# Two transform stages as 64x64 tiles: batches 2 to 7 of a Fourier mixing and feed-forward kernel

## The chip, the core and the metric

The kernel runs on one core of a Trainium2 chip. The core has a matrix engine (TensorE, "PE" in the profile, whose weight loads are shown apart as "PEld"), VectorE (DVE), ScalarE (ACT), GpSimd (POOL), a queue processor that here only issues transfers (SP), and sixteen DMA engines. The metric is the device time of one execution in microseconds (us); a kernel's time is the median of several runs.

## The reference

For every batch the sequence is filtered in the frequency domain, and the result goes through a two-layer network with a leaky ReLU:

```
x: (8, 3008, 256)    filt_r, filt_i: (1505, 256)    w_in: (256, 2048)    w_out: (2048, 256)
X = rfft(x, axis=1)
y = irfft(X * (filt_r + 1j * filt_i), n=3008, axis=1)
h = y.reshape(24064, 256) @ w_in
out = maximum(0.01 * h, h) @ w_out
```

## The kernel before

**The transform.** 3008 is 94 x 32, so each Fourier transform is made of two stages of small matrices. The kernel calls the four stages of a batch 1 to 4. Stage 1 (`s1_group`, line 254; its matmul is line 259) multiplies by the 94-point matrix: 16 groups a batch. Stage 2 (`s2_group`, line 302; matmul on line 308) multiplies by the 32-point matrix with the twiddle factors built in: 24 column blocks `c`, each with a weight matrix of its own (`f2_sb[:, c]`), 12 groups of two blocks a batch. Each block holds, on 128 partitions, the real and imaginary parts of two of the frequencies k1 side by side, and the weights are 128x128 with half of their entries zero, because the two frequencies do not mix. After stage 2 comes the product with the filter. Stage 3 (`sa_group`, line 326; matmul on line 330) goes back through the 32-point matrix, one matmul of 512 columns for each of the 12 groups, and its weights are again half zero. Stage 4 (`sb_group`, line 343; matmul on line 351) goes back through the 94-point matrix into `yt`, 16 groups a batch.

**The product with the filter.** It is complex: DVE multiplies the stage-2 result in PSUM by `fb_sb` into `p2` (line 317) and by `fa_sb` into `p1` (line 320); two transfers on SP swap the partition halves of `p2` into `p3` (lines 318 and 319), so that real parts meet imaginary parts; POOL adds `p1` and `p3` into `y` (line 323). `fb_sb` already holds the signs. The filter is loaded once at the start by POOL transfers that also convert float32 to float16 (line 204).

**Transposes.** Between stages 1 and 2 the data go through a DRAM tile `dz1` (stores from line 264, loads `t1_load`, line 268, into the ring `z1`), between stages 3 and 4 through `dz2` (stores from line 334, loads `t2_load`, line 275, into the ring `z2`). Both rings lie in the tile `big`.

**The network.** The 24064 tokens are taken in 47 chunks of 512. `moe1` (line 504) multiplies a chunk by `w_in`: 16 column tiles, two matmuls each (line 514), and after every second tile ACT applies the leaky ReLU to a pair of PSUM banks (line 519). The second layer is one chunk behind. From chunk 3 on it uses a seven-product scheme on quarters (matmuls of line 589; sums on DVE, lines 555 and 617 to 654).

**PSUM.** Two wide tiles (`ph`, two banks each) take turns for `moe1`. Two single banks (`pf`) serve the transform stages; `bank` (line 156) picks the one that by its own estimate (`frees`) comes free first. Two more hold the products of the second layer.

**The order.** The first batch is written out by hand as a list of steps (line 466). All that follows is put on a heap with a time and emitted in the order of these times (`at`, `work`). Time is counted in units, eight to a chunk. `plan` (line 694) gives each transform group of batches 1 to 7 a wished time; the loop from line 741 moves groups so that they stand at least `GAP` apart and after the transfers they need, with fixed allowances (`LANDED`, `READ`, `AFTER`). So each engine's order, and that of SP's and POOL's queues, is fixed when the program is built. An instruction whose data are late holds up everything behind it on its engine or queue.

In the first batch, stage 2 (`s2p`, line 390) also has matmuls with 128x64 weights, line 401: the two halves of the output partitions are made by two matmuls. Line 397 is the same with full weights.

Of the kernel before, what the change touches and what calls it, by code (L numbers as in the profile page):

```python
# [11 lines left out]
P = 128  # L12
FP16 = mybir.dt.float16
# [7 lines left out]
NC = 24  # L21
Q = 32
R1 = 96
FP = 3


def _build_np_constants(N):
    n1, n2 = np.arange(N1), np.arange(N2)
    h = N2 // 2

    k2 = np.concatenate([np.arange(h), np.arange(N2 - 1, h - 1, -1)])

    sg = np.where(k2 < h, 1.0, -1.0)[None, :]
    th = 2 * np.pi * np.outer(n2, k2) / N2
    co, si = np.cos(th), np.sin(th)

    fwd1 = np.zeros((P, P))
    fwd2 = np.zeros((P, NC, P))
    inv1 = np.zeros((P, N2, N1))
    inv2 = np.zeros((P, P))  # L40

    for s, (qr, qi) in enumerate(((0, 2), (1, 3))):
        k1 = NC * s + np.arange(NC)

        cr, ci = (slice(64 * i + s, 64 * i + 64, 2) for i in range(2))
        r, i = (slice(Q * q, Q * q + Q) for q in (qr, qi))
        ang = 2 * np.pi * np.outer(n1, k1) / N1
        fwd1[:N1, qr * Q : qr * Q + NC] = np.cos(ang)
        fwd1[:N1, qi * Q : qi * Q + NC] = -np.sin(ang)
        for c in range(NC):  # L50
            t = th + 2 * np.pi * n2[:, None] * k1[c] / N
            fwd2[r, c, cr], fwd2[i, c, cr] = np.cos(t), np.sin(t)
            fwd2[r, c, ci], fwd2[i, c, ci] = -np.sin(t) * sg, np.cos(t) * sg

        w = np.where((k1 == 0) | (k1 == N1 // 2), 1.0, 2.0)[:, None] / N1
        for j in n2:
            t = ang.T + 2 * np.pi * j * k1[:, None] / N
            inv1[qr * Q : qr * Q + NC, j, :] = w * np.cos(t)
            inv1[qi * Q : qi * Q + NC, j, :] = -w * np.sin(t)
        inv2[cr, r], inv2[ci, r] = co.T, -(si * sg).T  # L60
        inv2[cr, i], inv2[ci, i] = si.T, (co * sg).T
    inv2 /= N2


    inv2r = np.concatenate([inv2[:64], -inv2[:64]], axis=0)
    inv2i = np.concatenate([inv2[64:], inv2[64:]], axis=0)
    small = np.stack([fwd1, inv2, inv2r, inv2i], axis=1)

    fwd2t = fwd2.reshape(4, Q, NC, P).transpose(1, 0, 2, 3).reshape(P, NC, P)
    inv1t = inv1.reshape(4, Q, N2, N1)[:, :NC].transpose(1, 0, 2, 3).reshape(4 * NC, N2, N1)  # L70
    fwd2 = fwd2.reshape(P, FP, NC // FP, P).transpose(1, 0, 2, 3)
    return tuple(np.ascontiguousarray(t).astype(np.float16) for t in (fwd2, inv1, small, fwd2t, inv1t))


@with_exitstack
def kernel(
# [28 lines left out]
    REST = (5.37, 14.61, 8.86, 10.48, 23.53, 20.72)  # L105
    DUE = (3.52, 0.66)
    TWICE = (2.2, 2.35)
    F2T = 3.24
    LEAD = (3.85, 7.37)
    AFTER = (0.53, 0.8, 1.33, 3.17, 0.39, 0.52)  # L110
# [2 lines left out]
    PLANS = (  # L113
# [4 lines left out]
    )  # L118

    f2_np, i1_np, small_np, f2t_np, i1t_np = _build_np_constants(N)  # L120
    f2_d = nc.inline_tensor(f2_np, name="fwd2_const")
    i1_d = nc.inline_tensor(i1_np, name="inv1_const")
    small_d = nc.inline_tensor(small_np, name="small_const")
    f2t_d = nc.inline_tensor(f2t_np, name="fwd2t_const")
    i1t_d = nc.inline_tensor(i1t_np, name="inv1t_const")

    cpool = ctx.enter_context(tc.tile_pool(name="const", bufs=1))
    f2_sb = cpool.tile([P, NC, P], FP16, name="f2_sb")
# [3 lines left out]
    fb_sb = cpool.tile([P, NC, D], FP16, name="fb_sb")  # L132
    w_in_sb = cpool.tile([P, NDT, DFF], FP16, name="w_in_sb")
    w_out_sb = cpool.tile([P, NCT, D], FP16, name="w_out_sb")
    wt_sb = cpool.tile([P, 4, NCH, P], FP16, name="wt_sb")
    x_sb = cpool.tile([P, N2, D], FP16, name="x_sb")
    big = [cpool.tile([P, Q * D], FP16, name=f"big{i}") for i in range(3)]
# [31 lines left out]
    def at(time, f):  # L169
        clock["n"] += 1  # L170
        heapq.heappush(work, (time, clock["n"], f))
# [8 lines left out]
    def noted(what, f):  # L180
        f()
        issued.add(what)
# [58 lines left out]
    def turned(t, n, c):  # L241

        base = t[:]
        return bass.AP(tensor=base.tensor, offset=base.offset + 4 * c * D,
                       ap=[[P * D, n], [Q * D, 4], [1, 4 * D]])
# [22 lines left out]
    def t1_load(b, c):  # L268
        def go():
            need(*[("st1", b, h) for h in range(8)], *[("s2", b, 2 * c - 7)] * (c > 3))  # L270
            nc.sync.dma_start(z1[c % 4], turned(dz1[b % 2], N2, c))
            issued.add(("z1", b, c))
        return go

# [51 lines left out]
    def sa_group(b, g):  # L326
        def go():
            ps = bank("pf", 2, D)
            need(("y", b, g), *[("st2", b, g // 2 - 4)] * (g > 7))
            nc.tensor.matmul(ps, inv2, ys.pop((b, g))[:], start=True, stop=True)  # L330
            h = g // 2
            nc.scalar.copy(st2[h % 4][:, ds(2 * (g % 2), 2), :], ps)  # L332
            if g % 2:
                soon(AFTER[4], lambda: noted(("st2", b, h), lambda: nc.sync.dma_start(
                    dz2[b % 2][ds(4 * h, 4)].rearrange("k p d -> p k d"), st2[h % 4])))
        return go

    def quad_copy(h, dt, ps, copy):

# [164 lines left out]
    def moe1(ci, ct):  # L504
        g, j = divmod(ct, 2)
        if ct == 0:
            gts[ci] = gtp.tile([P, NCT, CH], FP16, tag="gt", name=f"gt_c{ci}")
        if j == 0:
            phs[0] = bank("ph", 2, CH)
        ph, t = phs[0], ci * CH  # L510
        while t < (ci + 1) * CH:
            e = min((ci + 1) * CH, (t // N + 1) * N)
            for dt in range(NDT):
                nc.tensor.matmul(ph[:, j, ds(t - ci * CH, e - t)], w_in_sb[:, dt, ts(ct, P)],  # L514
                                 yt[:, dt, ds(t % N, e - t)],
                                 start=(dt == 0), stop=(dt == NDT - 1))
            t = e
        if j == 1:
            nc.scalar.activation(gts[ci][:, ds(2 * g, 2), :], ph, AF.Lrelu)  # L519
# [174 lines left out]
    def plan(b, s1, s1_step, s2, s2_step, lag, sb, sb_step, xl, x_step):  # L694
        for g in range(16):
            groups.append((s1 + s1_step * g, 1, b, g, s1_group(b, g, dve if b == 1 and g % 4 < 3 else act)))
            if g % 2 and b + 1 < B:
                at(s1 + xl + x_step * g, lambda g=g: (need(("s1", b, g)), noted(
                    ("x", b + 1, g // 2), lambda: x_load(b + 1, 2 * g - 2, 4))))
        for g in range(12):  # L700
            groups.append((s2 + s2_step * g, 2, b, g, s2_group(b, g)))
            groups.append((s2 + lag + s2_step * g, 3, b, g, sa_group(b, g)))
        first_use[1, b], first_use[3, b] = s2, sb
        for g in range(16):
            due = SL * (QT * (8 * b + g // 2) // CH)
            groups.append((min(sb + sb_step * g, due - DUE[0] + DUE[1] * (g % 2)), 4, b, g, sb_group(b, g, act)))
# [21 lines left out]
    def load_time(stage, b, c):  # L728
# [7 lines left out]
            at(t, (t1_load if stage == 1 else t2_load)(b, c))  # L736
        return loads[stage, b, c]

    queue = [(time, n, *v) for n, (time, *v) in enumerate(groups)]
    heapq.heapify(queue)  # L740
    while queue:
        time, n, stage, b, g, f = heapq.heappop(queue)
        t = max(time, last + GAP)
        if stage == 3:
            behind = when[2, b, g] + y_delay(b, g) + 0.02 if (2, b, g) in when else None
        else:
            behind = load_time(stage - 1, b, g // 2) if stage != 1 else 0
            if stage != 1 and behind is not None:
                behind += READ
        if behind is None or behind + 0.02 > t:  # L750
            heapq.heappush(queue, (t + GAP if behind is None else behind + 0.03, n, stage, b, g, f))
            continue
        when[stage, b, g] = last = t
        at(t, f)
        if stage in (2, 4) and g % 2:
            place[stage - 1, g // 2 % 4] = t + 0.1
        assert stage < 4 or t < SL * (QT * (8 * b + g // 2) // CH), (b, g, t)

    for ci in range(NCHUNK + 1):
        if ci < NCHUNK:  # L760
            for ct in range(NCT):
                at(SL * ci + 0.5 * ct, lambda ci=ci, ct=ct: moe1(ci, ct))
        if ci == 0:
            continue
        wino = W0 <= ci - 1
        items = products(ci - 1) if wino else plain(ci - 1)
        for i, f in enumerate(items):
            at(SL * (ci + i / len(items)) + 0.01, f)
        if wino:
            for time, *what in [(v, i) for i, v in enumerate(SUMS)] if ci < NCHUNK else LAST:  # L770
                at(SL * ci + time, lambda ci=ci, what=what: act_sums(ci - 1, *what))
# [33 lines left out]
```

## Time and profile before

| | us |
|---|---|
| median of three runs | 748.61 |
| lowest and highest | 748.29, 750.29 |
| the profiled execution | 747.4 |
| its span, first to last instruction | 745.2 |
| granted TensorE clock | 0.999 of full |

The busy times of the profile's first part are unions over instructions. TensorE's matmuls are pipelined, so the mean duration of one is longer than its step in the stream. The chain of waits goes back from the last instruction to whatever released it; for a stream of matmuls it shows each one's step. DMA "share" is the mean busy share of the sixteen engines.

The groups that the change touches, beside those of lines 308 and 330, are these in the profile's list by form:

```profile
L332 ACT CAST big<-pf 128x512 f16<-128x512 f32 x84 | 49.0, 584 | 4.9 <-PE pf L330 3.0
L320 DVE TENSOR_TENSOR p_b_g<-pf,fa_sb 128x512 f32<-128x512 f32 x84 | 57.2, 681 | 0.2
L323 POOL TENSOR_TENSOR y_b_g<-p_b_g,p_b_g 128x512 f16<-128x512 f32 x84 | 116.4, 1388 | 414.9 <-DMA p_b_g<-p_b_g 249.9
```

The columns are the line, engine and operation, output and inputs, the count, the busy time with the mean in ns of one, and the engine's idle time just before with what ended most of it. There are 84 because batches 1 to 7 have twelve groups each.

### The profile page before, as it was taken

How to read it: one execution, taken by the hardware profiler on the slowest of the kernel's cores; microseconds unless marked ns; L12 is line 12 of the kernel's file. 1: busy time of each engine (PE TensorE's matmuls, PEld its weight loads, DVE VectorE, ACT ScalarE, POOL GpSimd, SP SyncE). 2: the span in 40 equal slices, each digit the busy share in tenths (PEclk: the TensorE clock that was granted, in tenths of full speed). 3: DMA queues.
4: the chain of work that ended last, by engine and by line, in shares of the span. 5: the costliest groups of instructions: out<-in, count | busy, mean ns of one | idle time of the engine just before them, and what ended most of it. 6: DMA issues, size and time to landing. Idle time of an engine off the chain costs nothing.

```text
span 745.2 us, 19416 instructions
## 1 busy us (share of the span) xinstructions
PE 738.0 (99%) x8017; PEld 528.9 (71%) x8017; DVE 504.6 (68%) x686; ACT 559.1 (75%) x755; POOL 166.2 (22%) x171
## 2 busy tenths in 40 slices
PE   9999999999999999999999999999999999999997
PEld 3556667677687777877778777777777777777776
DVE  5987637766776766766777667766677676465566
ACT  4776787888878787877777787787777777777762
POOL 6503412332232212121232222121212210000000
PEclk9999999999999999999999999999999999999999
DMA  9997797888876666655675656543554333111012
GB/s 207 229 224 197 191 224 216 209 195 208 216 181 147 159 186 176 169 138 163 193 178 150 159 155 175 156 139 109 144 160 119 106 103 103 60 55 55 29 46 70
DMA packets 119848, 113.64 MB, mean 152 GB/s; under 512 B 16384, under 2 KB 93056, under 8 KB 119568
## 3 DMA queue, kind: packets, MB, share of 16 engines
q1 hardware_dynamic: 104425, 94.73, 42.9%
q0 software_dynamic: 15056, 17.49, 15.8%
q8 instruction: 62, 1.02, 0.6%
q14 instruction: 26, 0.21, 0.1%
q10 hardware_dynamic: 279, 0.19, 0.1%
HBM read 57.51 MB, written 50.33 MB: 145 GB/s over the span
## 4 chain that ended last, share of the span: by engine, by line
PE 96%; DMA 1%; DVE 1%; ACT 1%; issue 0%; ACTq 0%; DVEq 0%
PE ph L514 43%; PE pf L589 18%; PE po_ps L589 18%; PE pf L259 3%; PE pf L351 3%; PE pf L308 2%; PE pf L330 2%; PE po_ps L373 1%; PE pf L681 1%; PE po_ps L681 1%; DMA dz<-big 1%; DMA big<-dz 0%; ACT yt L341 0%; PE pf L442 0%; PE ph L401 0%
## 5 line engine op out<-in xcount | busy, mean ns | idle before, releaser
L519 ACT ACTIVATE gt_c<-ph 128x1024 f16<-128x1024 f32 x376 | 385.3, 1025 | 133.5 <-PE ph L514 122.8
L514 PE MATMUL ph<-yt,w_in_sb 128*128 128x512 f16 (+7 forms) x1728 | 447.3, 351 | 0.2 <-ACT yt L341 0.2
L589 PEld LDWEIGHTS <-gt_c 128*128 128x128 f16 x2800 | 202.2, 98 | 91.1
L323 POOL TENSOR_TENSOR y_b_g<-p_b_g,p_b_g 128x512 f16<-128x512 f32 x84 | 116.4, 1388 | 414.9 <-DMA p_b_g<-p_b_g 249.9
L589 PEld LDWEIGHTS <-big 128*128 128x128 f16 x2128 | 151.2, 98 | 61.4
L514 PEld LDWEIGHTS <-w_in_sb 128*128 128x128 f16 x1728 | 137.5, 98 | 19.7 <-DVE yt L341 0.4
L317 DVE TENSOR_TENSOR p_b_g<-pf,fb_sb 128x512 f32<-128x512 f32 x78 | 53.7, 688 | 31.0 <-PE pf L308 13.8
L589 PE MATMUL po_ps<-wt_sb,gt_c 128*128 128x128 f16 x704 | 70.0, 219 | 0.0
L589 PE MATMUL pf<-wt_sb,gt_c 128*128 128x128 f16 x688 | 68.4, 219 | 0.0
L589 PE MATMUL pf<-w_out_sb,gt_c 128*128 128x128 f16 x720 | 67.9, 219 | 0.0
L589 PE MATMUL pf<-wt_sb,big 128*128 128x128 f16 x704 | 67.2, 219 | 0.0
L262 ACT CAST big<-pf 128x512 f16<-128x512 f32 x98 | 57.1, 588 | 11.9 <-PE pf L259 10.5
L589 PE MATMUL po_ps<-w_out_sb,gt_c 128*128 128x128 f16 x688 | 66.0, 219 | 0.0
L589 PE MATMUL po_ps<-wt_sb,big 128*128 128x128 f16 x688 | 65.3, 219 | 0.0
L341 ACT CAST yt<-pf 128x376 f16<-128x376 f32 x120 | 56.4, 473 | 10.9 <-PE pf L351 8.0
L555 DVE TENSOR_TENSOR big<-gt_c 128x2048 f16<-128x2048 f16 (+1 forms) x46 | 58.7, 1276 | 0.1
L555 DVE TENSOR_TENSOR gt_c<-gt_c 128x2048 f16<-128x2048 f16 x43 | 57.4, 1335 | 1.0
L320 DVE TENSOR_TENSOR p_b_g<-pf,fa_sb 128x512 f32<-128x512 f32 x84 | 57.2, 681 | 0.2
L555 DVE TENSOR_TENSOR big<-gt_c,big 128x2048 f16<-128x2048 f16 (+1 forms) x45 | 55.3, 1230 | 0.0
L555 DVE TENSOR_TENSOR big<-big,gt_c 128x2048 f16<-128x2048 f16 (+1 forms) x45 | 55.2, 1227 | 0.1
L332 ACT CAST big<-pf 128x512 f16<-128x512 f32 x84 | 49.0, 584 | 4.9 <-PE pf L330 3.0
L259 PE MATMUL pf<-x_sb,small_sb 94*128 94x512 f16 x109 | 41.6, 381 | 0.0
(97 smaller groups left out, 625.9 us busy)
## 6 DMA issues: line engine op xcount, KB each, us to landing
dz<-big SPq DMA_DIRECT2D x98, 256.0 KB
p_b_g<-p_b_g SPq DMA_DIRECT2D x156, 128.0 KB
out_dram<-ost_c_h SPq DMA_DIRECT2D x118, 128.0 KB
big<-dz SPq DMA_DIRECT2D x42, 256.0 KB
big<-dz SPq DMA_DIRECT2D x56, 192.0 KB
x_sb<-in_x_dram POOLq DMA_DIRECT2D x40, 192.0 KB, 4.4
x_sb<-in_x_dram POOLq DMA_DIRECT2D x2, 768.0 KB, 9.1
w_in_sb<-in_moe_w_in_dram POOLq DMA_DIRECT2D x1, 1024.0 KB, 13.2
```

The source lines that it names most:

```text
L259: nc.tensor.matmul(ps, fwd1[:N1], x_sb[:N1, ds(2 * g, 2), :], start=True, stop=True)
L262: copy(st[:, ds(2 * (g % 2), 2), :], ps)
L317: nc.vector.tensor_tensor(p2[:], ps, fb, AL.mult)
L320: nc.vector.tensor_tensor(p1[:], ps, fa, AL.mult)
L323: ("y", b, g), lambda: nc.gpsimd.tensor_tensor(y1[:], p1[:], p3[:], AL.add)))
L332: nc.scalar.copy(st2[h % 4][:, ds(2 * (g % 2), 2), :], ps)
L341: copy(yv, ps.rearrange("p c a -> p a c"))
L351: nc.tensor.matmul(ps[:, j, :], z2[h % 4][:K4, j, ts(dt, P)], i1_sb[:K4, 4 * h + j, :], start=True, stop=True)
L514: nc.tensor.matmul(ph[:, j, ds(t - ci * CH, e - t)], w_in_sb[:, dt, ts(ct, P)], yt[:, dt, ds(t % N, e - t)], start=(dt == 0), stop=(dt == ...
L519: nc.scalar.activation(gts[ci][:, ds(2 * g, 2), :], ph, AF.Lrelu)
L555: nc.vector.tensor_tensor(*(v[:, ds(c0, n)] for v in (o, i0, i1)), op)
L589: nc.tensor.matmul(of[t], a()[:, c, ts(t, P)], w[:, c, :], start=(c == 0), stop=(c == NCH - 1))
```

## The change

From batch 2 on (`QUARTERS`), stages 2 and 3 no longer multiply by half-empty 128x128 weights. The two frequencies of a block are multiplied apart, each with 64x64 weights, in the four quadrants of the matrix engine: the row half `s` is the frequency's partitions, the column half `par` one of two column blocks. A *visit* covers four blocks with two frequencies each, so eight small matmuls forward (`forward`), which stand for two of the former groups; in the same call the previous visit's blocks go backward (`backward`) in four matmuls of 512 columns. There are six visits a batch, at the fixed times `VISITS`, from batch 3 on one a chunk at 4.75 units, and one more that only goes backward. `forward` takes both `pf` banks, one for each `s`; `backward` takes a wide `ph` bank and is copied out by ACT as 128x1024.

Within a quadrant, real and imaginary rows now alternate, so the swap for the complex product goes between odd and even partitions. The filter must lie in another order for this: it is loaded a second time in two halves of the frequencies (`refills`), into the even partitions by POOL and from there to the odd ones by SP, and DVE multiplies `fb_sb` by an alternating sign. The new stage-2 weights go into the first half of `f2_sb`. The partition order of stage 1's output changes too (`qr, qi`), and `t1_load` reads `dz1` in a different order from batch 2 on. In the planning loop, other groups are kept away from visits by `AROUND`, and three column tiles of `moe1` after each visit are set later by `PAIRS`.

```diff
-    for s, (qr, qi) in enumerate(((0, 2), (1, 3))):
+    for s, (qr, qi) in enumerate(((0, 1), (2, 3))):
...
+    VISITS = (44.75, 49.75, 55.75, 60.75, 65.75, 71.75) + tuple(8 * c + 4.75 for c in range(9, 40))
+    AROUND = (0.8, 1.15, 2.1)
+    HOLDS = (1.0, 2.0)
+    PAIRS = (0.35, 0.1, 0.1)
+    SECOND = 1.05
+    ADDED = 1.4
+    STORED = 1.2
+    REFILLED = 1.7
...
-        (40.7, 1.73, 77.28, 3.57, 5.62, 130.03, 2.65, -0.23, 2.52),
+        (40.7, 1.93, 77.28, 3.57, 5.62, 130.03, 2.65, -0.23, 2.52),
...
-            nc.sync.dma_start(z1[c % 4], turned(dz1[b % 2], N2, c))
+            src = turned(dz1[b % 2], N2, c)
+            if b >= QUARTERS:
+                src = bass.AP(tensor=src.tensor, offset=src.offset, ap=[[Q * D, 4], [P * D, N2], [1, 4 * D]])
+            nc.sync.dma_start(z1[c % 4], src)
...
+    def refill(dst, src, q, par, k, first, sgn):
+        lo = H * par + Q * k
+        nc.gpsimd.dma_start(
+            halves(dst[lo : lo + Q, ts(q, NC // 2)])[0],
+            bass.AP(tensor=src.tensor, offset=src.offset + (first + sgn * (par + NC * q)) * D,
+                    ap=[[N1 * D, N2 // 2], [sgn * 2 * D, NC // 2], [1, D]]))
+
+    def both(t, q):
+        v = halves(t[:, ts(q, NC // 2)])
+        nc.sync.dma_start(v[1], v[0])
+
+    def signed(q):
+        v = fb_sb[:, ts(q, NC // 2)]
+        nc.vector.tensor_scalar(v, v, sign_sb[:], None, AL.mult)
+
+    def refills(q, t):
+        for n in range(8):
+            dst, src = ((fb_sb, filt_i), (fa_sb, filt_r))[n // 4]
+            at(t + 0.4 * n, lambda v=(dst, src, q, n // 2 % 2, n % 2, *((0, 1), (N1, -1))[n % 2]): refill(*v))
+        at(t + 4.2, lambda: both(fb_sb, q))
+        at(t + 5.6, lambda: both(fa_sb, q))
+        at(t + 7, lambda: signed(q))
+        if q == 0:
+            at(t, lambda: nc.sync.dma_start(sign_sb[:], sign_d.ap()))
+        else:
+            at(t, lambda: nc.sync.dma_start(i2q_sb[:], i2q_d.ap()))
+            at(t, lambda: noted(("f2q",), lambda: nc.sync.dma_start(f2q, f2q_d.ap())))
+
+    def forward(b, v):
...
+        ps = [bank("pf", 2, D, hold) for hold in HOLDS]
+        for j in range(2):
+            for s in range(2):
+                for par in range(2):
+                    c = 2 * j + par
+                    nc.tensor.matmul(ps[s][ts(par, H), j, :], f2q[ts(s, H), 4 * v + c, :],
+                                     z1[v % 4][ts(s, H), c, :], start=True, stop=True)
+        for s in range(2):
+            if s:
+                soon(SECOND, lambda: filtered(b, v, 1, ps[1]))
+            else:
+                filtered(b, v, 0, ps[0])
+
+    def filtered(b, v, s, ps):
+        p1, p2, p3 = (scrp.tile([P, 2, D], FP32, tag=f"p{i}", name=f"p{i}_b{b}_v{v}{s}") for i in (1, 2, 3))
+        nc.vector.tensor_tensor(p2[:], ps, fb2[:, s, ds(2 * v, 2), :], AL.mult)
+        a, o = halves(p2[:]), halves(p3[:])
+        for e in range(2):
+            soon(AFTER[1], lambda e=e: nc.sync.dma_start(o[1 - e], a[e]))
+        nc.vector.tensor_tensor(p1[:], ps, fa2[:, s, ds(2 * v, 2), :], AL.mult)
...
+        soon(ADDED, lambda: noted(("yq", b, v, s), lambda: nc.gpsimd.tensor_tensor(y[:], p1[:], p3[:], AL.add)))
+
+    def backward(b, v):
...
+        ps = bank("ph", 2, CH)
+        y = [ys.pop((b, v, s)) for s in range(2)]
+        for par in range(2):
+            for s in range(2):
+                nc.tensor.matmul(ps[ts(s, H), par, :], i2q_sb[ts(par, H), :],
+                                 y[s][ts(par, H)].rearrange("p j d -> p (j d)"), start=True, stop=True)
+        nc.scalar.copy(st2[v % 4].rearrange("p (j w) d -> p w j d", w=2), ps.rearrange("p w (j d) -> p w j d", j=2))
...
+    def visit(i):
+        b, v = QUARTERS + i // 6, i % 6
+        if b < B:
+            forward(b, v)
+        if i:
+            backward(b - (v == 0), (v - 1) % 6)
...
+        for v in visits:
+            if -AROUND[0] < t - v < AROUND[1] or AROUND[1] < t - v < AROUND[2] and last > v:
+                t = v + AROUND[1 if last < v else 2]
...
+    for q in range(2):
+        refills(q, when[2, 1, 5 + 6 * q] + REFILLED)
+
+    later = {}
+    for t in visits[1:]:
+        for n, v in enumerate(PAIRS):
+            later[2 * int(t) + 2 + n] = v
...
-                at(SL * ci + 0.5 * ct, lambda ci=ci, ct=ct: moe1(ci, ct))
+                at(SL * ci + 0.5 * ct + later.get(NCT * ci + ct, 0), lambda ci=ci, ct=ct: moe1(ci, ct))
```

More of the change, by code (lines that the diff above doesn't have):

```diff
@@ L23 @@
 R1 = 96
+H = 64
 FP = 3
@@ L40, in _build_np_constants @@
     inv2 = np.zeros((P, P))
-    for s, (qr, qi) in enumerate(((0, 2), (1, 3))):
+    fwd2q = np.zeros((P, NC, H))
+    inv2q = np.zeros((P, H))
+    for s, (qr, qi) in enumerate(((0, 1), (2, 3))):
         k1 = NC * s + np.arange(NC)
@@ L53, in _build_np_constants @@
             fwd2[r, c, ci], fwd2[i, c, ci] = -np.sin(t) * sg, np.cos(t) * sg
+            fwd2q[r, c, 0::2], fwd2q[i, c, 0::2] = np.cos(t), np.sin(t)
+            fwd2q[r, c, 1::2], fwd2q[i, c, 1::2] = -np.sin(t) * sg, np.cos(t) * sg
         w = np.where((k1 == 0) | (k1 == N1 // 2), 1.0, 2.0)[:, None] / N1
@@ L61, in _build_np_constants @@
         inv2[cr, i], inv2[ci, i] = si.T, (co * sg).T
+        re, im = (slice(H * s + e, H * s + H, 2) for e in range(2))
+        inv2q[re, :Q], inv2q[im, :Q] = co.T / N2, -(si * sg).T / N2
+        inv2q[re, Q:], inv2q[im, Q:] = si.T / N2, (co * sg).T / N2
     inv2 /= N2
@@ L71, in _build_np_constants @@
     fwd2 = fwd2.reshape(P, FP, NC // FP, P).transpose(1, 0, 2, 3)
-    return tuple(np.ascontiguousarray(t).astype(np.float16) for t in (fwd2, inv1, small, fwd2t, inv1t))
+    return tuple(np.ascontiguousarray(t).astype(np.float16) for t in (fwd2, inv1, small, fwd2t, inv1t, fwd2q, inv2q))
 @with_exitstack
@@ L107 @@
     TWICE = (2.2, 2.35)
+    QUARTERS = 2
+    VISITS = (44.75, 49.75, 55.75, 60.75, 65.75, 71.75) + tuple(8 * c + 4.75 for c in range(9, 40))
[6 more added lines that the diff above has]
+    REFILLED = 1.7
     F2T = 3.24
@@ L115 @@
         (12.19, 1.53, 42.87, 2.62, 7.4, 85.59, 2.85, 16.13, 2.12),
[1 row of a table removed]
[1 row of a table added]
         (63.95, 2.85, 119.86, 3.87, 7.04, 177.42, 2.92, 12.93, 2.24),
     )
-    f2_np, i1_np, small_np, f2t_np, i1t_np = _build_np_constants(N)
+    f2_np, i1_np, small_np, f2t_np, i1t_np, f2q_np, i2q_np = _build_np_constants(N)
     f2_d = nc.inline_tensor(f2_np, name="fwd2_const")
@@ L125 @@
     i1t_d = nc.inline_tensor(i1t_np, name="inv1t_const")
+    f2q_d = nc.inline_tensor(f2q_np, name="fwd2q_const")
+    i2q_d = nc.inline_tensor(i2q_np, name="inv2q_const")
+    sign_d = nc.inline_tensor(np.where(np.arange(P) % 2, -1.0, 1.0).astype(np.float32)[:, None], name="sign_const")
     cpool = ctx.enter_context(tc.tile_pool(name="const", bufs=1))
@@ L134 @@
     w_out_sb = cpool.tile([P, NCT, D], FP16, name="w_out_sb")
+    i2q_sb = cpool.tile([P, H], FP16, name="i2q_sb")
+    sign_sb = cpool.tile([P, 1], FP32, name="sign_sb")
     wt_sb = cpool.tile([P, 4, NCH, P], FP16, name="wt_sb")
@@ L336, in sa_group, with halves @@
         return go
+    f2q = f2_sb[:].rearrange("p (a c) m -> p a c m", a=2)[:, 0].rearrange("p c (e m) -> p (c e) m", e=2)
+    fa2, fb2 = (f[:].rearrange("p (s j) d -> p s j d", s=2) for f in (fa_sb, fb_sb))
+    def halves(v):
+        return v.rearrange("(k e) j d -> e k j d", e=2)
+    def refill(dst, src, q, par, k, first, sgn):
[4 more added lines that the diff above has]
+                    ap=[[N1 * D, N2 // 2], [sgn * 2 * D, NC // 2], [1, D]]))
@@ new lines, in forward @@
+    def forward(b, v):
+        need(("z1", b, v), ("f2q",))
+        for g in (2 * v, 2 * v + 1):
+            issued.add(("s2", b, g))
+        ps = [bank("pf", 2, D, hold) for hold in HOLDS]
[10 more added lines that the diff above has]
+                filtered(b, v, 0, ps[0])
@@ new lines, in filtered @@
+    def filtered(b, v, s, ps):
[5 more added lines that the diff above has]
+        nc.vector.tensor_tensor(p1[:], ps, fa2[:, s, ds(2 * v, 2), :], AL.mult)
+        ys[b, v, s] = y = ypp.tile([P, 2, D], FP16, tag="y", name=f"y_b{b}_v{v}{s}")
+        soon(ADDED, lambda: noted(("yq", b, v, s), lambda: nc.gpsimd.tensor_tensor(y[:], p1[:], p3[:], AL.add)))
@@ new lines, in backward @@
+    def backward(b, v):
+        need(("yq", b, v, 0), ("yq", b, v, 1), *[("st2", b, v - 4)] * (v > 3))
+        ps = bank("ph", 2, CH)
[5 more added lines that the diff above has]
+        nc.scalar.copy(st2[v % 4].rearrange("p (j w) d -> p w j d", w=2), ps.rearrange("p w (j d) -> p w j d", j=2))
+        soon(STORED, lambda: noted(("st2", b, v), lambda: nc.sync.dma_start(
+            dz2[b % 2][ds(4 * v, 4)].rearrange("k p d -> p k d"), st2[v % 4])))
@@ L699, in plan @@
                     ("x", b + 1, g // 2), lambda: x_load(b + 1, 2 * g - 2, 4))))
[L700 to L703, printed above, removed]
+        if b < QUARTERS:
+            for g in range(12):
+                groups.append((s2 + s2_step * g, 2, b, g, s2_group(b, g)))
+                groups.append((s2 + lag + s2_step * g, 3, b, g, sa_group(b, g)))
+        first_use[1, b], first_use[3, b] = s2 if b < QUARTERS else VISITS[6 * (b - QUARTERS)] - 1, sb
         for g in range(16):
@@ L737, in load_time @@
         return loads[stage, b, c]
+    visits = VISITS[: 6 * (B - QUARTERS) + 1]
+    for i, t in enumerate(visits):
+        at(t, lambda i=i: visit(i))
+        for g in range(2):
+            when[2, QUARTERS + i // 6, 2 * (i % 6) + g] = t
+    for b in range(QUARTERS, B):
+        when[3, b, 11] = visits[6 * (b - QUARTERS) + 6] + STORED - AFTER[4]
     queue = [(time, n, *v) for n, (time, *v) in enumerate(groups)]
@@ L757 @@
         assert stage < 4 or t < SL * (QT * (8 * b + g // 2) // CH), (b, g, t)
+    for i, t in enumerate(visits):
+        b, v = QUARTERS + i // 6, i % 6
+        if b < B:
+            ready = load_time(1, b, v)
+            assert ready is not None and ready + READ < t, (b, v, ready, t)
+            place[1, v % 4] = t + 0.1
+    for q in range(2):
[4 more added lines that the diff above has]
+            later[2 * int(t) + 2 + n] = v
     for ci in range(NCHUNK + 1):
```

## The prediction

> **What bounds the kernel now.** I read the busy shares first, then the chain of waits, then the groups by form.
>
> ```profile
> PE 738.0 (99%) x8017; PEld 528.9 (71%) x8017; DVE 504.6 (68%) x686; ACT 559.1 (75%) x755; POOL 166.2 (22%) x171
> PE 96%; DMA 1%; DVE 1%; ACT 1%; issue 0%; ACTq 0%; DVEq 0%
> L308 PE MATMUL pf<-big,f_sb 128*128 128x256 f16 x168 | 32.1, 273 | 0.2 <-ACT big L262 0.2
> L330 PE MATMUL pf<-y_b_g,small_sb 128*128 128x512 f16 x84 | 31.8, 379 | 0.0
> ```
>
> TensorE is busy 99% of the span and is 96% of the chain that ends last; the two stages that change wait 0.2 us in all. So a microsecond taken out of TensorE's stream is a microsecond off the time, and any new wait of TensorE is added to it whole. Group durations (273, 379 ns) are latencies of overlapping matmuls; the price of one in the stream is its step in the chain. The chain's shares are 2.5% for L308 and 2.4% for L330, that is 18.6 us / 168 = 111 ns and 17.9 us / 84 = 213 ns (256 and 512 columns at the granted clock of 0.999).
>
> The chain's first stretch shows what the tiled matmuls of the first batch cost:
>
> ```profile
> 18.07 0.35 PE pf L401 x8
> 18.43 0.23 PE ph L401 x8
> 18.66 0.34 PE pf L397 x4
> ...
> 19.45 0.23 PE pf L397 x4
> ```
>
> L401 runs 128x64 column tiles, 128 columns each, two halves in turn. Eight that follow others of their kind take 0.23 us, so two halves run at once (eight in a row would be 8 x 55 ns = 0.44 us) and a load with its matmul costs 28 ns. Eight that follow full tiles take 0.35 us: going into the tiled form costs 0.12 us. Four full tiles after them take 0.34 us instead of 0.23: going out costs 0.11 us.
>
> Last, the place where TensorE is already just in time:
>
> ```profile
> 100.69 5.51 DMA dz<-big
> 106.21 2.98 DMA big<-dz
> 109.24 0.35 PE L351 MATMUL pf<-i_sb,big 96*128 96x94 f16 x4 [0.16 <-DMA big<-dz]
> 95.00:105.00 10.00, 10.00 (x87) 6.35 (x86) 5.54 (x6) 9.61 (x16) 1.98 (x4) 1.00 1.04 233
> x_sb<-in_x_dram POOLq DMA_DIRECT2D x6, 192.0 KB, 6.7
> q1 hardware_dynamic: 5132, 4.05, 55.7%
> q0 software_dynamic: 672, 1.18, 31.7%
> ```
>
> The first two lines are the chain: batch 1's last store to dz2 lands 5.51 us after its issue, the load of z2 takes 2.98 us more, and the first L351 of batch 1 waits 0.16 us for it (the timeline's line). There is no slack there. The fourth line is the stretch of 95 to 105 us: the DMA engines' share is 1.04, at 233 GB/s. The last three are the transfers of 85 to 110 us: a load from POOL lands after 6.7 us, and the queues hold 87% of the engines' time.
>
> **The change, part by part.** *Removed from TensorE:* a visit stands for two groups, so four L308 and two L330: 4 x 111 + 2 x 213 = 0.87 us. Six batches of six: 36 x 0.87 = 31.3 us.
>
> *Added to TensorE:* eight 64x64 matmuls of 256 columns forward and four of 512 backward, one after the other in the code, so one entry and one exit a visit. No row shows row tiles running beside each other. Bounds: four quadrants at once (2 x 256 + 512 columns: 0.21 + 0.21 us; at 28 ns a pair of load and matmul the eight need 0.23), or two at once as L401 shows (in a row all twelve are 8 x 111 + 4 x 213 = 1.74 us, so 0.87 us). I take four, because L401's two halves overlap without loss and the quadrants here share no rows, bank or partitions. Forward 0.23, backward 0.22, in and out 0.23 (0.26 from the repeating L401/L425 stretch, as the upper end): 0.68 us. There are 37 visits, the first only forward and the last only backward: 36 x 0.45 + 37 x 0.23 = 24.7 us. **Net: 24.7 - 31.3 = -6.6 us.**
>
> On weight loads a rule speaks against this. The Trainium skill, TensorEngine Tiling (Array Packing), Restrictions, says that column tiling turns fast weight load off; TensorE: Matmul & The Clock Gate, LDWEIGHTS, gives columns / 1.2 ns for one load, so by my estimate from that page twelve loads of 64 columns in a row are 0.64 us, a visit 0.87 us and the net about +0.2 us. L401's eight loads and eight matmuls in 0.23 us say that such loads overlap, and I go by them.
>
> *ACT:* twelve copies of 584 ns a batch (L332) become six of about 1025 ns (L519's shape), 0.9 us less. They now go through the wide banks that the up-projection uses. After a visit the next up-projection reuses the bank filled just before it. From the start of that last pair to its fill's end is 0.59 us (L514 x2), then 1.025 us of ACT and some 0.1 us of hand-over: 1.7 us. TensorE's work between, in the middle batches' order: 0.43 + 4 x 0.055 + 0.68 + 8 x 0.055 = 1.77 us. It fits by 0.07 us while ACT is free; the moved up-projection matmuls (0.35 of a unit, about 0.7 us) make that room. If ACT is still in a 0.58 us copy, TensorE waits up to 0.5 us.
>
> *DVE and POOL:* the same number of products (681 and 688 ns), swaps and additions; the second half's products start 1.05 units later, and each narrow bank is free again before the next group of the plan (about 2 us of TensorE work later, two products being 1.4 us). Two sign products of 128x3072 are new: L714, half as many partitions and as many columns, took 958 ns, so 0.96 us each, in DVE's 32% of idle time. If DVE must wait for the filter there, the additions behind it (L639 to L653's kind) hold the output banks, and TensorE's products wait for those.
>
> *The filter's reload, once:* 16 transfers on POOL of 96 KB (issue 0.54 to 0.73 us, as L196 and L204: 9 to 12 us of a queue that is 22% busy), four copies of 384 KB and two constants (384 and 16 KB) on SP. Half of it falls between about 93 us and the first visit. On SP the copies stand ahead of batch 1's first z2 loads, and each waits for its four POOL transfers. The last of these stands at unit 33.2 of the plan; batch 1's first L351 stands at unit 38.5 and ran at 109.2 us, unit 0 at 34.3 us, so a unit is 1.95 us here and the transfer is due at 99 us. With 0.5 us of issue and 6.7 us to land it arrives at 106.2 us, the copy's issue takes 0.5 us, and z2, which was issued at 106.21, goes out at about 106.7: 0.4 to 0.5 us late at least. The upper bound is bandwidth. The second half is 8 x 96 KB on q0 (107 engine-us a MB from the lines above: 85) and 1.2 MB on q1 (55 engine-us a MB: 66): 151 / 16 = 9.4 us of all engines, where the stretches from 91 to 121 us leave about 4.4 us free (nearly all of it from 105 to 115). So up to 5 us late. TensorE waits that much once, at the first L351 of batch 1, or before it for the output banks that a blocked DVE holds; the two waits overlap. I take the middle, **+2.7 us**.
>
> **Sum:** -6.6 + 2.7 = -3.9 us. The profiled run took 747.4 us (span 745.2 and 2.2 around it), 1.2 below the median of 748.61: 747.4 - 3.9 = 743.5, and at the median **744.7 us**. Its own range: a late z2 of 0.4 to 5 us and switches of up to 0.26 give 742.4 to 748.1.
>
> **Rivals.**
> 1. *Three quadrants' worth of overlap.* Loads and issue might hold the four apart. Matmul time is 1.74 / 3 = 0.58 us, a visit 0.81: 36 x 0.06 - 0.23 = 1.9 us gained, 2.7 lost: 749.4. For it: twelve separate loads a visit. Against: L401. The Trainium skill, TensorE: Matmul & The Clock Gate, Part 3, has 6.32 times for nine tiles, about 0.7 of the ideal; by that estimate four tiles give 2.8. No run here shows it yet.
> 2. *Row halves one after the other* (the change does not do what it says). A visit is 0.87 + 0.23 = 1.10 us: 36 x 0.23 + 0.23 = +8.5, +2.7: 759.8, slower. It decides as soon as fewer than two and three quarters run at once (1.74 / 0.64, where 0.64 + 0.23 is the 0.87 us taken out). For it: no row-tiled matmul in the trace. Against: different banks and partitions throughout.
> 3. *A wait on ACT in place of the matmuls.* If every second visit meets a 0.5 us wait for the wide bank: 18 x 0.5 = 9 us, 753.7. The point is 0.18 us a visit. For it: 0.07 us of slack, ACT at 75%. Against: the plan keeps other groups at least 0.8 units away before a visit.
> 4. *The reload floods the DMA engines.* By packets instead of bytes (1,536 of 512 B at 127 engine-us / 672 = 0.19 us) q0's part is 290 engine-us, 22 us with q1's: z2 would be late by some 9 us even if half of that is hidden: 751.0. Against: a packet of a third of the bytes should cost less.
>
> **How the numbers follow.** Forecast 0.66; rivals 0.10, 0.07, 0.08 and 0.09. Within 0.3% is 746.4 to 750.9, about what a measurement of this kernel can tell from no change. Of the forecast's 0.66, 0.55 lies below 746.4 and the rest within; a better overlap of the reload under the rivals adds 0.02 to faster. The first rival is mostly within (0.08 of 0.10), the fourth half. So faster 0.57, same 0.21, slower 0.22. The range is 741.0 to 752.0: it holds the forecast, the first rival and most of the fourth, and leaves the second, most of the third and the tails out.
>
> **What would show it.** A visit's step in the chain: 0.65 to 0.75 us for both lines together, not 0.8 or 1.1; entry and exit of 0.12 and 0.11. TensorE's idle time before the first L351 of batch 1 (or at the output banks just before) of 0.4 to 5 us, released by a transfer. No idle time at the up-projection after visits. I am wrong if visits take over 0.87 us, if TensorE waits at most visits, or if the reload's wait passes 6.6 us.

## The result, and the profile after

The changed kernel takes 789.9 us (median of 4 runs, 789.29 to 791.8), against 748.45 us for the kernel before on the same chip: a ratio of 1.0557, 95% interval 1.0526 to 1.0588. The forecast was 744.7 us. The profiled execution has a span of 790.0 us.

The first lines of the page after (busy shares; then the chain of waits by engine and by line):

```profile
PE 748.1 (95%) x8233; PEld 525.4 (67%) x8233; DVE 522.6 (66%) x688; ACT 553.1 (70%) x719; POOL 176.4 (22%) x187
PE 79%; DMA 14%; SPq 2%; DVE 1%; POOL 1%; issue 1%; ACT 1%; POOLq 0%; DVEq 0%; ACTq 0%
```

TensorE was 96% of the chain and is 79%; transfers were 1% and are 14%. The list of who made TensorE wait (total us, times, longest) names them:

```profile
PE pf L456 <- DMA big<-dz: 17.8, 5, 4.7
PE ph L430 <- POOL y_b_v L422: 9.1, 5, 6.4
PE pf L281 <- DMA x_sb<-in_x_dram: 3.6, 1, 3.6
PE pf L406 <- DMA big<-dz: 3.1, 1, 3.1
...
PE pf L355 <- DVE p_b_g L345: 0.8, 1, 0.8
```

Line 456 is the matmul of stage 4, 430 a visit's backward half, 406 its forward half, 281 stage 1, and 355 stage 3 of batch 1, which still has the 128x128 weights. Together this is 34 us of waiting where the kernel before had under 1 (1.7 us in the first batch, the same in both kernels, left aside). The visits themselves are as cheap as forecast. In the chain of after, around 417 us:

```profile
417.65 0.34 PE pf L406 x8
417.99 0.22 PE ph L430 x4
418.20 0.55 PE pf L694 x8
```

Eight forward matmuls take 0.34 us with the way in, four backward 0.22, and eight full tiles of line 694 after them 0.55 instead of 8 x 0.055 = 0.44: 0.11 for the way out. A visit costs 0.67 us; 0.68 was forecast. So all four quadrants run at once, row halves too, and separate weight loads do not hold them up.

The wait of batch 4 at line 456, in the same chain (start, length, what; SPq is SP's own queue):

```profile
390.08 13.33 DMA big<-dz
...
404.75 4.62 DMA dz<-big
...
409.39 2.80 DMA big<-dz
...
412.24 0.35 PE pf L456 x4
...
413.12 0.85 PE ph L619 x2
```

The first line is the last of four z1 loads, which lands 13.33 us after its issue. SP issues six output stores and a fifth z1 load in that time; the swap for the filter product and the store of stage 3 that stand behind them in its queue go out only after the landing. The store's own landing and the z2 load follow, and TensorE has waited 4.16 us. The last line shows what comes on top: two matmuls of line 619 of 512 columns take 0.85 us instead of 0.43. The granted clock by stretch says why (columns: stretch, length, busy us of PE, PEld, DVE, ACT and POOL, clock, DMA share, GB/s):

```profile
412.00:413.00 1.00, 0.76 (x10) 0.77 (x11) 0.00 (x0) 0.38 (x1) 1.00 (x3) 0.73 0.91 294
413.00:414.00 1.00, 1.00 (x7) 0.45 (x5) 0.00 (x0) 0.10 (x1) 1.00 (x3) 0.50 0.96 151
414.00:415.00 1.00, 1.00 (x9) 0.73 (x8) 0.29 (x1) 0.00 (x0) 0.14 (x1) 0.50 0.93 178
415.00:416.00 1.00, 1.00 (x9) 0.72 (x8) 1.00 (x2) 0.39 (x1) 0.00 (x0) 0.56 1.11 256
416.00:417.00 1.00, 1.00 (x13) 0.69 (x11) 0.26 (x1) 0.63 (x1) 0.00 (x0) 1.00 1.07 265
```

After this wait the clock is at half for some 3.4 us, so about 1.7 us of work is lost besides the wait. Seven waits are of over 3 us. Five are followed by 3.4 us at half; around the other two it is 6.8 and 10 us (a mean clock of 0.66 from 107 to 117 us and of 0.61 from 141 to 154 us). That is some 34 us at half, and up to 17 us lost.

### The profile page after: what moved, and what is told of

It reads as the page before. It is cut to its first block, busy times and chain, and to the rows that moved or that the text cites. A ratio compares the mean times of both kernels' runs of the same rounds, so it can differ in the third digit from the quotient of the medians.

```text
span 790.0 us, 19821 instructions
## 1 busy us (share of the span) xinstructions
PE 748.1 (95%) x8233; PEld 525.4 (67%) x8233; DVE 522.6 (66%) x688; ACT 553.1 (70%) x719; POOL 176.4 (22%) x187
## 4 chain that ended last, share of the span: by engine, by line
PE 79%; DMA 14%; SPq 2%; DVE 1%; POOL 1%; issue 1%; ACT 1%; POOLq 0%; DVEq 0%; ACTq 0%
PE ph L619 35%; PE pf L694 15%; PE po_ps L694 15%; DMA big<-dz 7%; DMA dz<-big 5%; PE pf L456 2%; PE pf L281 2%; DMA p_b_v<-p_b_v 2%; PE po_ps L478 1%; PE pf L786 1%; PE pf L406 1%; PE po_ps L786 1%; PE ph L430 1%; POOL y_b_v L422 1%; SPq L419 1%
## 5 line engine op out<-in xcount | busy, mean ns | idle before, releaser
L619 PE MATMUL ph<-yt,w_in_sb 128*128 128x512 f16 (+7 forms) x1728 | 454.4, 356 | 0.2 <-ACT yt L446 0.2
L422 POOL TENSOR_TENSOR y_b_v<-p_b_v,p_b_v 128x512 f16<-128x512 f32 x72 | 102.3, 1424 | 419.8 <-DMA p_b_v<-p_b_v 222.8
L694 PEld LDWEIGHTS <-big 128*128 128x128 f16 x2128 | 147.2, 99 | 69.2 <-issue 13.3
L284 ACT CAST big<-pf 128x512 f16<-128x512 f32 x98 | 57.1, 584 | 15.0 <-PE pf L281 13.9
L660 DVE TENSOR_TENSOR big<-gt_c 128x2048 f16<-128x2048 f16 (+1 forms) x46 | 63.7, 1384 | 0.3
L660 DVE TENSOR_TENSOR gt_c<-gt_c 128x2048 f16<-128x2048 f16 x43 | 60.3, 1402 | 1.4
L416 DVE TENSOR_TENSOR p_b_v<-pf,fb_sb 128x512 f32<-128x512 f32 x72 | 49.4, 686 | 11.3 <-PE pf L406 7.8
L456 PE MATMUL pf<-i_sb,big 96*128 96x94 f16 x448 | 38.9, 209 | 17.8 <-DMA big<-dz 17.8
L420 DVE TENSOR_TENSOR p_b_v<-pf,fa_sb 128x512 f32<-128x512 f32 x72 | 49.0, 680 | 0.0
L432 ACT CAST big<-ph 128x1024 f16<-128x1024 f32 x36 | 36.3, 1008 | 13.6 <-PE ph L430 13.6
```

The source lines that it names most:

```text
L284: copy(st[:, ds(2 * (g % 2), 2), :], ps)
L416: nc.vector.tensor_tensor(p2[:], ps, fb2[:, s, ds(2 * v, 2), :], AL.mult)
L420: nc.vector.tensor_tensor(p1[:], ps, fa2[:, s, ds(2 * v, 2), :], AL.mult)
L422: soon(ADDED, lambda: noted(("yq", b, v, s), lambda: nc.gpsimd.tensor_tensor(y[:], p1[:], p3[:], AL.add)))
L432: nc.scalar.copy(st2[v % 4].rearrange("p (j w) d -> p w j d", w=2), ps.rearrange("p w (j d) -> p w j d", j=2))
L456: nc.tensor.matmul(ps[:, j, :], z2[h % 4][:K4, j, ts(dt, P)], i1_sb[:K4, 4 * h + j, :], start=True, stop=True)
```

## The experiments

**The order of the z1 loads, alone.** My first theory after the result: the new order has an outermost size of 4, and a transfer is shared out over the DMA engines by that size, so these loads run on four of sixteen. The Trainium skill, DMA: Bandwidth & Descriptors, the section on why a DMA increments its semaphore by 16, gives the rule: the number of engines is the largest up to 16 that divides the outermost size (other than 1) of both sides. The run below agrees, with a share of 0.26 of the sixteen engines. The kernel before, with the load changed from batch 2 on:

```diff
-            nc.sync.dma_start(z1[c % 4], turned(dz1[b % 2], N2, c))
+            src = turned(dz1[b % 2], N2, c)
+            if b >= 2:
+                src = bass.AP(tensor=src.tensor, offset=src.offset, ap=[[Q * D, 4], [P * D, N2], [1, 4 * D]])
+            nc.sync.dma_start(z1[c % 4], src)
```

> The kernel before, with the new order of the z1 loads alone from batch 2 on (four quarters outermost, 32 rows within), so that rows of stage 2's input stand in other partitions than its weights expect: the numbers of batches 2 to 7 are not the reference's, the work is the same. Theory 1: a load whose outermost size is 4 runs on four DMA engines; four of them take 11 to 13 us instead of 4, and everything that SP issues behind them lands late. Then this kernel is slower by 20 to 45 us: 768 to 793, with about four packets of 2048 B in flight during these loads. Rival (the visits, the reload and their waits cost the time): within 1% of before, 742 to 756.

It took 793.6 us, 1.0605 (1.0582 to 1.0628) times the kernel before. In its chain, the swap that SP issues behind four such loads lands after 10 us:

```profile
276.03 2.30 SPq L321
...
278.38 10.04 DMA p_b_g<-p_b_g
...
288.58 1.27 POOL y_b_g L326
```

A batch later the case is the same: four z1 loads are issued from 371.74 us on, the swap behind them at 374.77, and it lands at 387.25; TensorE stands still for it. The DMA share of 384 to 388 us in forty slices, in tenths, and then the first 1.6 us of that as one stretch (DMA share and GB/s are its last columns):

```profile
DMA  2323232323232323453432231223232322323232
384.00:385.60 1.60, 0.00 (x0) 0.00 (x0) 0.00 (x0) 0.00 (x0) 0.00 (x0) 1.00 0.26 102
```

A share of 0.26, with transfers waiting, is what four busy engines of sixteen give (4 / 16 = 0.25). In the kernel before, a burst of the same loads, with a swap behind them, moves at 0.95:

```profile
355.00:356.00 1.00, 1.00 (x12) 0.65 (x11) 0.35 (x1) 1.00 (x2) 0.00 (x0) 1.00 0.95 313
```

For each busy engine that is 20.6 GB/s (313 / (0.95 x 16)), and 24.5 in the slow stretch (102 / (0.26 x 16)). So the transfers are not slower there; fewer engines work at once. The profile does not number the engines: that there are four is read from the share.

**The changed kernel with the old order.** The `if b >= QUARTERS` branch of `t1_load` is taken out.

> The changed kernel with the old order of the z1 loads throughout (32 rows outermost, quarters within): stage 2 gets its rows in another order than its weights expect, so batches 2 to 7 are not the reference's; the work is the same. Theory 1: 741 to 750, a visit's 0.67 us unchanged, and the waits of 3 to 5 us at the first matmul of stage 4 gone in batches 3 to 7. Rival (visits and reload): still above 775.

It took 755.6 us, ratio 1.0097 (1.0082 to 1.0112). So 34.3 us of the loss come from the order of the loads. The visits stay at 0.34 + 0.22 us, and the waits of batches 3 to 6 at stage 4 are gone. But it missed the expected 741 to 750: 11 us over the forecast were still to be explained. Its waits:

```profile
PE pf L454 <- DMA big<-dz: 5.1, 1, 5.1
PE pf L281 <- DMA x_sb<-in_x_dram: 3.2, 1, 3.2
PE ph L428 <- POOL y_b_v L420: 1.4, 1, 1.4
...
PE pf L353 <- DVE p_b_g L343: 0.8, 1, 0.8
```

The first two stand at 119 and 110 us, where the filter is reloaded. In the chain there, batch 1's stores to dz2 land after 9 to 10 us (5.51 before):

```profile
96.14 9.20 DMA dz<-big
...
105.41 9.76 DMA dz<-big
...
115.62 3.51 DMA big<-dz
```

**Without the reload.** The old order, and `refill`, `both` and `signed` taken out of `refills`.

> As the kernel with the old order of the z1 loads, and without the filter's second load: its 16 transfers, four copies and two sign products are left out, so batches 2 to 7 are multiplied by the filter in the first order. If the reload costs 2.7 us once, as predicted: 2 to 4 us faster than the kernel with the old order alone. If the reload is hidden: within 1 us of it. The forecast for this kernel is 740 to 746.

743.3 us, ratio 0.9934 (0.9917 to 0.9950): 0.7% faster than the kernel before, and 12.2 us faster than with the reload (the ratios' difference, 0.0163, of 747.8). The forecast for this kernel held; the expected 2 to 4 us for the reload did not.

**The same data by other transfers.** A pattern with 32 rows outermost can't put the quarters one after the other in one transfer. Four transfers of 32 partitions can:

```diff
-            nc.sync.dma_start(z1[c % 4], src)
+            for q in range(4 if b >= QUARTERS else 0):
+                nc.sync.dma_start(z1[c % 4][ts(q, N2)].rearrange("n j d -> n (j d)"), bass.AP(
+                    tensor=src.tensor, offset=src.offset + q * Q * D, ap=[[P * D, N2], [1, 4 * D]]))
```

> The changed kernel with each z1 load of batches 2 to 7 as four loads of 32 partitions (one for each quarter, 32 rows outermost): the same data in the same places as in the changed kernel. Theory 1: every engine takes part again, but SP issues 36 x 3 more transfers of about 0.5 us: 742 to 758. Rival: above 775.

773.0 us, ratio 1.0348 (1.0296 to 1.0401): better than the changed kernel, but outside the expectation. SP issues the sixteen loads of a batch's start one after the other, 8.47 us in a row:

```profile
375.68 8.47 SPq L297 DMA_DIRECT2D big<-dz  x16
```

Two transfers of 64 partitions (32 rows outermost, then two quarters), with the rows of the 64x64 weights in the same order, cost less of SP:

```diff
+            for s in range(2 if b >= QUARTERS else 0):
+                nc.sync.dma_start(z1[c % 4][ts(s, H)], bass.AP(
+                    tensor=src.tensor, offset=src.offset + 2 * s * Q * D, ap=[[P * D, N2], [Q * D, 2], [1, 4 * D]]))
...
+    fwd2q = fwd2q.reshape(2, 2, Q, NC, H).transpose(0, 2, 1, 3, 4).reshape(P, NC, H)
```

> The changed kernel with each z1 load of batches 2 to 7 as two loads of 64 partitions (32 rows outermost, then two quarters, so all engines can take part), the rows of the 64x64 weights put in the same order. Theory (four loads cost 17 us over the old order by their 108 extra transfers on SP): a third as many extra transfers, so 755.6 + 17.5 / 3 = 757 to 764. Rival (the cost of many loads is the shorter partition range and not SP's queue): 768 or more.

753.6 us, ratio 1.0085 (1.0070 to 1.0100): no slower than the old order in one transfer, below what was expected. After 165 us TensorE no longer waits over 0.3 us anywhere. So SP's queue does not charge by the transfer: eight issues in a row fit. That the row of sixteen is what cost the 17.5 us is likely, but not shown; the transfers of 32 partitions were not tried without it.

**Two loads, without the reload.** The same part left out as above.

> The changed kernel with two loads for each z1 load, and without the filter's second load (its transfers, copies and sign products left out, so batches 2 to 7 are multiplied by the filter in the first order). If the two loads cost nothing once all engines take part, this equals the old order without the reload, 743.3 within 1.5 us, and the reload costs the 10 us between this and two loads with it. If SP's 36 extra transfers cost something when nothing else does: 745 to 748.

744.9 us, ratio 0.9961 (0.9948 to 0.9974). That is 1.6 us above the old order without the reload (2.0 by the ratios), so neither quite the 1.5 us expected for loads that cost nothing nor the 745 to 748 of the rival. Against the two loads with the reload, the reload costs 0.0124 of 748 us, 9.3 us. TensorE still waits 0.5 to 1.2 us three times, for batch 1's z2 and at two early visits.

**Moving the reload.** The filter's columns are ordered by visits instead of by frequency, so that the second half is needed only by the fourth visit, and it is issued from unit 45.5 on; the first half goes out at half the rate.

```diff
-        refills(q, when[2, 1, 5 + 6 * q] + REFILLED)
+        refills(q, (when[2, 1, 5] + REFILLED, 45.5)[q])
...
-        nc.vector.tensor_tensor(p2[:], ps, fb2[:, s, ds(2 * v, 2), :], AL.mult)
+        nc.vector.tensor_tensor(p2[:], ps, fb_sb[:, ds(12 * (v // 3) + 6 * s + 2 * (v % 3), 2), :], AL.mult)
```

> As the kernel with two loads, and the reload split by visits instead of by frequencies: its first half (visits 0 to 2) issued at half the rate, its second half (visits 3 to 5) only after the first visit, at unit 45.5, when the DMA engines' share is 0.6 to 0.75 instead of 1.0 to 1.2. Theory (the reload's 12 us are transfers that meet batch 1's last stores and batch 3's x in a full DMA stretch, and the lower clock after the waits): 8 to 12 us faster than with two loads alone, 746 to 753. Rival (the reload costs its own work wherever it stands): within 3 us of two loads alone.

751.7 us, ratio 1.0052 (1.0037 to 1.0067): 2 us better, not 8 to 12, as the rival had it. The wait for x is gone and that for z2 is 2.25 us, but visits now wait 2.11, 0.68 and 1.40 us for POOL's additions, at 137 to 162 us. With the second load on POOL:

> As the kernel before it, with the second of the two loads issued by POOL instead of SP. If SP's queue is what the extra loads cost: 743 to 748, faster than both loads on SP by 2 to 6 us. If POOL's additions are held up behind the loads: slower than both on SP.

757.4 us, 1.0126 (1.0109 to 1.0143): worse. A forward half waits 4.13 us for its z1 load at 199 us. The late reload with the old order in one transfer:

> The old order of the z1 loads in one transfer (rows in another order than the weights expect, so batches 2 to 7 are not the reference's), with the late reload. It shows what the visits give when neither the loads nor the reload stand in the way: between 743.3 (without any reload) and 748, so the reload costs under 4 us. Rival (the reload costs its work wherever it stands): 753 or more.

750.1 us, 1.0033 (1.0022 to 1.0044), near the kernel before, but between what was expected and the rival's 753. Two more attempts to get the reload out of the way. First, the tiles only from batch 3 on:

> Two loads for each z1 load, the reload split by visits, and the 64x64 tiles from batch 3 on instead of batch 2: the reload's first half then starts after batch 2's sixth stage-2 group (unit 58), its second half at unit 84, and all visits are a chunk apart. Thirty visits save 30 x 0.19 = 5.7 us less 0.2 for the last one. Theory (what is left of the loss comes from the crowded transfers up to about 165 us and from visits only five units apart): waits of TensorE under 1 us in all after the first batch, and 742 to 745. Rival (a reload costs 2 us or more wherever it stands): 746 to 750, with the waits moved to 140 to 190 us.

754.5 us, 1.0073 (1.0054 to 1.0092); the runs spread from 750.9 to 759.8. Beside 2.58 us for batch 1's z2 at 112 us, the waits moved to 191 to 217 us, the longest again 5.71 us for a z2 load. The time is above both ranges. Then, from batch 2 on again, an earlier first visit and a slower second half:

> As two loads with the late reload, the first visit one unit earlier (43.75), so that six units lie between it and the second, and the reload's second half at a lower rate with a pause for the additions on POOL. Theory (what is left is 2.1 us for z2 and 4.2 us of waits for POOL's additions at the second to fourth visit): those waits fall to 1 to 2 us and the time to 747 to 750. Rival (the transfers themselves are late, wherever POOL stands): 751 to 753, as before.

753.1 us, 1.0075 (1.0049 to 1.0101): the waits for the additions, 1.42, 1.28, 1.06 and 1.82 us, did not fall. The time is at the upper edge of the rival's range. In both, as their rivals said, the transfers are late, wherever they stand in the first 220 us. None of the versions with the whole computation beats the kernel before.

## Why the prediction was wrong

*The visits* were right: 0.67 us against 0.68, entry and exit included, four quadrants at once. Rivals 1 and 2 (partial overlap, row halves in turn) are out, and so is the visit of 0.87 us. That one was estimated from the Trainium skill, TensorE: Matmul & The Clock Gate, LDWEIGHTS. The trace does not bear that estimate out: eight loads and eight matmuls, way in included, take 0.34.

*The wait on ACT* (rival 3) did not come: ACT releases no wait over 0.3 us in the changed kernel; the 0.07 us of slack worked out for it were enough.

*The step that failed is one that the prediction left out.* Its list of parts goes from the filter's reload straight to the sum; the z1 loads' new order, which stands in the diff and in the text ahead, got no price, as if the same bytes in the same number of transfers cost the same. They cost 34.3 us (789.9 to 755.6 with the order undone; 45.9 when put into the kernel before alone). The mechanism: four engines instead of sixteen, four loads at a batch's start that need over 10 us instead of an estimated 3.4 (1 MB at the 313 GB/s of the burst in the kernel before), everything that SP issues behind them late, then two waits: POOL's additions and z2. Of the 35.9 us between the two spans, TensorE's waits over 0.3 us account for 23.4 (34.5 against 11.1 after the first batch). The mean granted clocks, 0.977 and 0.995, make up to 14 us more, some of it inside the waits, which covers the other 12.5. I had not looked for a price of a pattern's order.

*The reload* was priced too low: 2.7 us forecast with 5 as its upper bound, 9.3 to 12.2 measured. The fourth rival's 9 us was nearer, but by luck, for its reason does not show. These are the packets of POOL's queue in the old order, with the reload and without (packets, MB, share of 16 engines):

```profile
q0 software_dynamic: 18384, 19.06, 16.8%
q0 software_dynamic: 15056, 17.49, 15.3%
```

Over spans of 754.1 and 743.5 us that is some 210 engine-us more (140 against the kernel before). The price by bytes, 2 x 85 = 170 for both halves, fits this; the rival's price by packets, 2 x 290 = 580, does not. What was mis-sized is how late z2 goes out. The prediction let batch 1's last store leave and land as before. In the old-order run it leaves at 105.41 us instead of 100.69, released in the chain by a store that took 9.20 us, and lands after 9.76 instead of 5.51. So z2 is issued at 115.62, 9.4 us later than before; 0.4 to 5 was forecast. The DMA share from 103 to 115 us is 1.25 and then 1.16 where it was 0.72 and 0.68; that the crowding alone makes the stores slow is argued, not shown.

Two things were left out. The wait for x at stage 1 (3.2 us) is a second victim beside z2. And the clock falls with the wait for z2: 0.92 and 0.74 in the two stretches between 110 and 130 us, where it was 1.00.

*The sum without both* held. The old order without the reload is 4.5 us faster than the kernel before by the medians (4.9 by the ratio), where 6.6 was worked out. Its profiled run is the slowest of the four, 1.7 us shorter in span than the kernel before. Waits of 1.84 us at z2 and of 1.52, 0.54 and 0.32 us at early visits, 4.2 us in all, would leave 2.4 of the 6.6, so the two agree within 0.7 us.

What would have shown it wrong hardly came: visits take 0.67 us, TensorE waits over 0.3 us at five of 37 of them, and the waits at the reload (3.62 us for x and 1.56 for z2) stay under 6.6 us. Only in the old-order run do these two pass it together, at 8.3 us. Most of the 41 us came from a load whose price I had not asked.

## What to carry to other kernels

Ask of every changed access pattern what its outermost size is on both sides: a transfer with four rows of anything outermost kept about four of sixteen DMA engines busy here, at 102 GB/s where a burst in the other order moved 313, and held up what its queue issued behind it. A DMA share that stays at a quarter while an engine waits for a transfer is the sign. And where TensorE has no slack, price a one-time reload by every transfer that it meets, and reckon with some lost clock after a wait of about 2 us or more. The length of the wait alone does not decide it, as the last point below shows.

## What was not expected of the hardware

- Splitting a 256 KB load into two cost nothing measurable with the reload (753.6 against 755.6 us) and some 2 us without it (0.9961 against 0.9934 of the kernel before, at the edge of the noise); into four, 17.5 us (773.0 against 755.6).
- The four quadrants ran at the ideal rate (0.22 us for four matmuls of 512 columns, 0.85 one after the other), with a switch of 0.11 us out of the tiled form.
- After a wait of 4.16 us the granted clock was 0.5 for about 3.4 us. So it was after one of 2.25 us (two loads, late reload: a mean of 0.79 from 112 to 120 us), but not after one of 3.17 us (old order: 1.00 from 109 to 115 us). Waits of up to 1.84 us (old order without the reload) left its mean at 0.999.
